# A planned FFT and feed-forward kernel: new piece lengths in its planner, and group 6 prepared tile by tile

## The chip, the core and the metric

The kernel runs on one core of a Trainium2 chip. The metric is the device time of one execution in microseconds (us). Three runs of the kernel before took 1422.62, 1423.76 and 1426.18 us, so the median is 1423.76 us. The profile is of one more execution, which took 1424.53 us; its span, from the first instruction to the last, is 1422.7 us.

## The reference

There are 8 batches of 3136 tokens with 256 channels, all in float32. The reference filters each batch along the tokens in the frequency domain, adds to the result the real part of its two-dimensional Fourier transform, normalizes each token, and sends it through two matrix products with a rectifier between them:

```python
X = np.fft.rfft(x, axis=1)
y = np.fft.irfft(X * (filt_r + 1j * filt_i)[None], n=3136, axis=1)
mixed = np.real(np.fft.fft(np.fft.fft(y, axis=1), axis=2))
u = y + mixed
un = (u - mean(u)) / sqrt(var(u) + 1e-6)
out = u + np.maximum(un @ w_ch1, 0) @ w_ch2    # 256 -> 1024 -> 256
```

## The kernel before

**The stages.** A batch goes through `load_x`, `first` (the first step of the transform, 14 pieces, stored to DRAM as `d1`), `load_at` (`d1` read back turned, 7 pieces, tile `at`), `spectrum` (the second step on TensorE from `at`, then the filter), `inverse1` and `inverse2` (the way back, through DRAM as `d2` and `dy`), and `fold`, which makes the input of the channel transform (`eo`). By symmetry a batch holds 1568 rows of two tokens. The rows of all batches stand in one line and are cut into 49 groups of 256 rows. A group is two tiles of 128 rows, and `pages` holds its tokens.

**A group.** `fetch(g)` reads the group from DRAM. `prepare(g)` mixes the channels on TensorE (`mixing`, the `mix` matmuls of L1081), and adds the result to the group: tile 0 on VectorE (`add`, L1106), tile 1 on GpSimd (`add_plain`, L1131 to L1137, from a copy `sm` that ScalarE makes at L1169). Then come the statistics of each tile (L1246, L1247), the scale and shift in `weigh` (L1215 on ScalarE, L1219 to L1227 on VectorE), and `normalize`, once for each tile: ScalarE writes the normalized tile `un` (L1277), ScalarE and a second engine split it into two float16 halves `u` (L1297 and L1303, GpSimd for most groups), and a DMA transpose on SP's queue turns it into `ut` (L1306). Group 0 goes another way. Its two tiles are finished, weighed and normalized by two tasks of their own (`tile_alone`), and TensorE turns `un` (L1283, `uT`), after which ScalarE and VectorE write the halves straight into `ut` (L1287, L1289). For every other group the one task finishes tile 0, then tile 1, then weighs both together.

**The products.** One task, `products`, runs 8 steps for a group, 392 in all. Step q multiplies the group's `ut` with an eighth of the first weights (`h`, L1328, six matmuls), and then the rectified `h` of two steps before with the second weights (`acc`, L1369, twelve matmuls). It waits for both tiles of `ut` before the first product of a group, so the second products of the last two steps of the group ahead stand behind that wait. `rectify` (L1356 on ScalarE, L1358 on VectorE) turns a first product into the operand of a second one.

**The planner.** No engine chooses its next instruction at run time: each runs its own in the order in which they were written. That order comes from the class `Plan`, which plays the whole kernel through on a clock of its own before anything is built. A task yields an engine and a length (`yield "DVE", 0.65`), and whichever waiting piece has the lowest order number goes next when its engine comes free. `HOP` is the time that the planner adds when a task goes from one engine to another. An SP piece takes its length on the modelled DMA engines. Buffers are rings that a task asks for with `take`. Four banks of PSUM (`psf`) are shared by `first`, `spectrum`, `inverse1`, `inverse2` and the channel mix.

**Order numbers.** Step q of the products has order q. `prepare(g)` has 8g - 19 and `normalize(g, t)` has 8g - 13 + t, so 29 and 35 + t for group 6. The spectra of batch 2 start at 47.45, and step 48 is the first of group 6. Group 6 is the one with the first row of batch 1 in it (row 1568, the group has 1536 to 1791), and its scale factors come from two batches (`alpha_of`, small copies at L1068 and L1070).

## Time and profile before

| | |
|---|---|
| median of three runs | 1423.76 us |
| profiled execution | 1424.53 us |
| span of the profiled execution | 1422.7 us |
| mean granted TensorE clock | 0.972 of full speed |
| TensorE matmuls busy | 1347.1 us, 95% |
| VectorE busy | 1024.7 us, 72% |
| ScalarE busy | 865.0 us, 61% |
| GpSimd busy | 666.5 us, 47% |
| DMA engines, share of 16 | 77.9% |

PE is TensorE's matmuls and PEld its weight loads, DVE is VectorE, ACT ScalarE, POOL GpSimd, and SPq the sequencer that issues the DMAs. A busy share is a mean over stages that have different limits. "idle before <- releaser" says what ended the idle time ahead of an instruction. The granted clock is 1.00 at 2.4 GHz and 0.50 at 1.2 GHz.

### The profile page before, as it was taken

What the parts mean: (1) busy time and instruction counts of PE and PEld (TensorE: products, weight loads), DVE (VectorE), ACT (ScalarE), POOL (GpSimd) and SP (SyncE); (2) the same over time, 40 slices, a digit from 0 to 9 for tenths busy, and PEclk for the clock granted to TensorE, in tenths of its full rate; (3) what the DMA queues carried; (4) which work ended last, traced back from release to release, by engine and by line L of the source; (5) the groups of instructions that cost most, each with busy time, mean ns of one, the idle gap of its engine ahead of it and who ended that gap; (6) DMA issues with size and microseconds to landing.
All of it is one profiled execution on the core that took longest, in us unless ns stands there. A gap on an engine that the chain in (4) does not pass through costs nothing.

```text
span 1422.7 us, 32916 instructions
## 1 busy us (share of the span) xinstructions
PE 1347.1 (95%) x12637; PEld 910.9 (64%) x12637; DVE 1024.7 (72%) x2178; ACT 865.0 (61%) x1647; POOL 666.5 (47%) x827
## 2 busy tenths in 40 slices
PE   5758999969999999999999999999999999999998
PEld 2634666646766676667666666666666676666666
DVE  5687588787778696877779776786968778454543
ACT  4466468746776477756677557755667566444341
POOL 2521295057822585338642675336742597222120
PEclk8767999989999999999999999999999999999999
DMA  9997888887985989689896998669795998544330
GB/s 274 241 285 202 188 187 225 239 211 161 215 224 143 229 192 245 182 183 182 224 209 176 215 226 208 179 163 223 169 262 151 209 207 187 151 109 131 84 78 30
DMA packets 362702, 270.30 MB, mean 190 GB/s; under 512 B 217984, under 2 KB 298320, under 8 KB 362544
## 3 DMA queue, kind: packets, MB, share of 16 engines
q1 hardware_dynamic: 362544, 268.19, 77.9%
q8 instruction: 99, 1.62, 0.5%
q14 instruction: 59, 0.48, 0.1%
HBM read 114.50 MB, written 102.76 MB: 153 GB/s over the span
## 4 chain that ended last, share of the span: by engine, by line
PE 47%; DVE 4%; ACT 2%; DMA 2%; POOL 1%; issue 1%; SPq 1%; POOLq 0%; ACTq 0%; DVEq 0%
PE acc L1369 20%; PE h L1328 19%; PE s L607 2%; PE y L978 2%; PE mix L1081 1%; PE i L890 1%; DMA x<-x 1%; DVE pages L1106 1%; PE s L721 1%; PE s L722 1%; DVE h L1358 1%; DVE st L1246 1%; DMA at<-d 0%; ACT h L1356 0%; DVE x L584 0%
## 5 line engine op out<-in xcount | busy, mean ns | idle before, releaser
L1369 PE MATMUL acc<-w2s,h 128*128 128x256 f16 x4704 | 587.3, 273 | 1.0 <-DVE pages L1383 0.7
L1328 PE MATMUL h<-ut,w1s 128*128 128x512 f16 x2352 | 574.7, 380 | 3.4 <-ACT ut L1287 1.7
L1369 PEld LDWEIGHTS <-h 128*128 128x128 f16 x4704 | 452.1, 98 | 133.0 <-issue 10.9
L1358 DVE SCALAR_TENSOR_TENSOR h<-h,h 128x512 f16<-128x512 f32 x392 | 268.7, 686 | 232.8 <-ACT h L1356 230.6
L1356 ACT ACTIVATE h<-h 128x512 f16<-128x512 f32 x392 | 233.3, 595 | 309.4 <-PE h L1328 299.1
L1328 PEld LDWEIGHTS <-w1s 128*128 128x128 f16 x2352 | 224.5, 98 | 210.4 <-issue 16.6
L1303 POOL TENSOR_TENSOR u<-un,u 128x512 f16<-128x512 f32 x94 | 110.7, 1179 | 315.8 <-ACT u L1297 287.0
L1277 ACT ACTIVATE un<-pages,sb 128x256 f32<-128x256 f32 x196 | 110.9, 596 | 16.7 <-DVE sb L1227 16.6
L1131 POOL TENSOR_TENSOR pages<-sm,pages 128x508 f32<-128x508 f32 x48 | 61.5, 1282 | 112.2 <-ACT sm L1169 78.9
L782 POOL TENSOR_TENSOR late<-yt,late 128x448 f16<-128x448 f32 x98 | 102.8, 1054 | 17.4 <-ACT late L780 16.5
L831 POOL TENSOR_TENSOR eo<-ef,eo 128x448 f16<-128x448 f32 (+6 forms) x62 | 59.6, 966 | 97.0 <-ACT eo L828 68.6
L754 POOL TENSOR_TENSOR yt<-yt,t 128x224 f32<-128x224 f32 x98 | 64.9, 662 | 66.4 <-DVE t L740 51.3
L740 DVE SCALAR_TENSOR_TENSOR t<-s,pF,ft 128x448 f32<-128x448 f32 x126 | 84.0, 675 | 10.2 <-PE s L722 9.7
L1106 DVE SCALAR_TENSOR_TENSOR pages<-mix,alpha,pages 128x254 f32<-128x254 f32 (+2 forms) x188 | 83.9, 478 | 8.9 <-ACT sm L1169 7.5
L1003 ACT ACTIVATE ys<-y,alpha 128x512 f32<-128x512 f32 x110 | 70.9, 683 | 31.8 <-PE y L978 31.6
L1246 DVE BATCH_NORM_STATS2 st<-pages 128x6 f32<-128x256 f32 x196 | 80.5, 411 | 6.5 <-POOL pages L1137 4.9
L740 DVE SCALAR_TENSOR_TENSOR yt<-s,pF,ft 128x448 f32<-128x448 f32 x98 | 66.3, 676 | 25.4 <-PE s L722 22.0
L1383 DVE SCALAR_TENSOR_TENSOR pages<-acc,beta,pages 128x512 f32<-128x512 f32 x98 | 70.4, 743 | 15.7 <-PE acc L1369 15.6
L721 PE MATMUL s<-s,at 112*128 112x56 f16 x896 | 61.5, 190 | 19.9 <-DMA at<-d 17.6
L935 POOL TENSOR_TENSOR bt<-sd,bt 128x512 f16<-128x512 f32 x42 | 48.6, 1159 | 62.7 <-ACT bt L933 62.6
L780 ACT CAST late<-yt 128x448 f16<-128x448 f32 x98 | 55.1, 563 | 33.5 <-POOL yt L756 26.2
L584 DVE SCALAR_TENSOR_TENSOR x<-x,sx,x 112x512 f16<-112x512 f32 x84 | 70.1, 857 | 4.3 <-ACT x L582 4.2
(164 smaller groups left out, 1736.5 us busy)
## 6 DMA issues: line engine op xcount, KB each, us to landing
x<-x SPq DMA_DIRECT2D x56, 448.0 KB
d<-ast SPq DMA_DIRECT2D x112, 224.0 KB
at<-d SPq DMA_DIRECT2D x56, 448.0 KB
pages<-d SPq DMA_DIRECT2D x112, 224.0 KB
out<-pages SPq DMA_DIRECT2D x98, 256.0 KB
pages<-dy SPq DMA_DIRECT2D x92, 256.0 KB
d<-bt SPq DMA_DIRECT2D x98, 224.0 KB
dy<-ys SPq DMA_DIRECT2D x96, 224.0 KB
```

The costliest lines, as they stand in the source:

```text
L721: nc.tensor.matmul(o, w, s2[:, U, 0].rearrange("p (r k) -> p r k", r=2), start=True, stop=False)
L740: nc.vector.scalar_tensor_tensor(out, p, pF[:, 1:2], f, op0=ALU.mult, op1=ALU.mult)
L782: nc.gpsimd.tensor_tensor(y16v[:, 1], yh, y16v[:, 0], op=ALU.subtract)
L1003: nc.scalar.activation(ys[:, 2 * o : 2 * o + 2], p, AF.Copy, scale=alphas[b][:, 2:3])
L1106: nc.vector.scalar_tensor_tensor(out, p, al, y, op0=ALU.mult, op1=ALU.add)
L1246: nc.vector.bn_stats(st[:, 2 * t + k], y[:, t, k])
L1277: nc.scalar.activation(un[:, k], y[:, t, k], AF.Identity, bias=sb[:, i, 1:2], scale=sb[:, i, 3:4])
L1303: nc.gpsimd.tensor_tensor(u16[:, :, :, 1], unv, u16[:, :, :, 0], op=ALU.subtract)
L1328: nc.tensor.matmul(p.rearrange("p (t k q) -> p t k q", t=2, k=2), w1s[:, d, hw, 128 * f : 128 * f + 128], utv[:, :, :, d, hx], start=i == ...
L1356: nc.scalar.activation(h[:, 0], p, AF.Relu)
L1358: nc.vector.scalar_tensor_tensor(h[:, 1], p, 0.0, h[:, 0], op0=ALU.max, op1=ALU.subtract)
L1369: nc.tensor.matmul(acc[:, kind], h[:, hh, c0 : c0 + 128], w2s[:, f, hw], start=f == 0 and kind == 0 and i == 0, stop=f == 7 and kind == 1 ...
```

## The change

Two things are changed. First, the lengths that tasks tell the planner, and `HOP`, get other values. The list is long; most lengths of VectorE and ScalarE go down by 5 to 10%, a few go up, and `HOP` goes from 0.1 to 0.18. These numbers only decide the order in which the instructions are written on each engine and queue; no instruction is added or taken away by them. Second, group 6 is prepared as group 0 is: each of its tiles by a task of its own, with order numbers 13 and 14 (15 and 16 for `normalize`), and turned by TensorE in a bank of the ring `psf`. So for group 6 one `weigh` over four columns becomes two over two columns, and for each tile a ScalarE cast, a GpSimd subtraction and a DMA transpose become four TensorE transposes, a ScalarE copy and a VectorE subtraction. Its ring entry for `ut` is taken before the tiles are finished and not after.

```diff
+ALONE = (0, 6)
+TURNED = (0, 6)
-HOP = 0.1
+HOP = 0.18
...
-            yield "ACT", 0.67
+            yield "ACT", 0.62
...
-            yield "DVE", 0.72
+            yield "DVE", 0.8
...
-            yield "PE", 0.66
+            yield "PE", 0.69
...
-            yield "SP", 1.95, t + max(0, ch - 2)
+            yield "SP", 2.0, t + max(0, ch - 2)
...
-        yield "PE", 0.4 if b else 0.6
+        yield "PE", 0.43 if b else 0.6
...
-        yield "DVE", 0.66
+        yield "DVE", 0.6
...
-            yield "DVE", 0.7
+            yield "DVE", 0.67
...
-        yield "POOL", 1.15
+        yield "POOL", 1.3
...
-            plan.spawn(normalize(g, t, y, sb, ut), -56 + t)
+            plan.spawn(normalize(g, t, y, sb, ut), 8 * g + FIRST + 2 + t - 20 if g else -56 + t)
 
         kt = None
-        if g == 0:
+        if g in ALONE:
             kt = yield take("ut")
             ut = mp.tile([128, 2, 8, 128], F16, tag="ut", name=f"ut_{g}", bufs=2)
             ready[g] = y, ut, kt
             for t in range(2):
-                plan.spawn(tile_alone(t), -55 + t)
+                plan.spawn(tile_alone(t), 8 * g + FIRST - 20 + t if g else -55 + t)
             return
...
-        if g == 0:
-            kp = yield take("pso")
-            pt = ps_o.tile([128, 4, 128], F32, tag="pso", name=f"uT_{t}")
+        if g in TURNED:
+            ring = "psf" if g else "pso"
+            kp = yield take(ring)
+            pt = bank(f"uT_{g}_{t}") if g else ps_o.tile([128, 512], F32, tag="pso", name=f"uT_{t}")
+            pt = pt.rearrange("p (i q) -> p i q", i=4)
             yield "PE", 0.7
...
-                yield "PE", 1.3, q
+                yield "PE", 1.312, q
...
-                    yield "PE", 0.655, q + 0.5
+                    yield "PE", 0.664, q + 0.5
...
-        yield "ACT", 0.54
+        yield "ACT", 0.5
         nc.scalar.activation(h[:, 0], p, AF.Relu)
-        yield "DVE", 0.65
+        yield "DVE", 0.605
```

## Rows read from the trace of the kernel before

**Rows 1.** The head of the page: the span, and the busy time of each engine with its share of the span and its instructions.

```profile
span 1422.7 us, 32916 instructions
...
PE 1347.1 (95%) x12637; PEld 910.9 (64%) x12637; DVE 1024.7 (72%) x2178; ACT 865.0 (61%) x1647; POOL 666.5 (47%) x827
```

**Rows 2.** Busy time by stretches of the span: from and to, its length, busy us and instructions of each engine, the granted clock, the DMA share and GB/s.

```profile
0.00:130.00 130.00, 80.32 (x570) 50.25 (x570) 95.46 (x213) 73.65 (x149) 41.69 (x60) 0.74 0.94 264
130.00:275.00 145.00, 143.16 (x1319) 93.56 (x1319) 113.02 (x227) 97.75 (x185) 65.14 (x84) 1.00 0.84 197
275.00:325.00 50.00, 38.51 (x364) 26.41 (x362) 38.48 (x95) 24.65 (x49) 24.92 (x34) 0.90 0.92 228
325.00:1400.00 1075.00, 1066.04 (x10254) 727.36 (x10252) 770.15 (x1635) 665.20 (x1261) 534.79 (x650) 1.00 0.77 181
```

**Rows 3.** What TensorE waited for between 260 and 340 us: us in total, times, the longest.

```profile
PE s L721 <- DMA at<-d: 9.7, 1, 9.7
PE s L607 <- DVE pages L1106: 1.6, 1, 1.6
```

**Rows 4.** TensorE in order of time from 294 to 314 us: start, length, the operation, and in brackets the idle time before it. The line at 305.34 is the first of the 32 matmuls of two spectra of batch 2, of which the other 31 are left out; 306.83 is the first step of group 6; 309.37 and 312.44 are the last two second products of group 5.

```profile
294.72 0.95 PE L1081 MATMUL mix<-mix,eo 128*128 128x129 f16 x16
305.34 0.23 PE L721 MATMUL s<-s,at 112*128 112x56 f16 x1 [9.66 <-DMA at<-d]
...
306.83 2.74 PE L1328 MATMUL h<-ut,w1s 128*128 128x512 f16 x6
309.37 1.94 PE L1369 MATMUL acc<-w2s,h 128*128 128x256 f16 x12
311.14 1.46 PE L1328 MATMUL h<-ut,w1s 128*128 128x512 f16 x6
312.44 1.47 PE L1369 MATMUL acc<-w2s,h 128*128 128x256 f16 x12
```

**Rows 5.** Busy time in stretches of 2 us, with the columns of rows 2; the third number from the end is the granted clock.

```profile
287.00:289.00 2.00, 0.38 (x3) 0.24 (x3) 1.98 (x5) 0.35 (x1) 0.00 (x0) 1.00 0.38 137
...
299.00:301.00 2.00, 0.00 (x0) 0.00 (x0) 0.80 (x2) 1.10 (x3) 2.00 (x3) 0.77 0.51 133
...
309.00:311.00 2.00, 2.00 (x13) 1.41 (x12) 1.93 (x3) 0.72 (x2) 2.00 (x3) 0.67 1.25 275
311.00:313.00 2.00, 2.00 (x15) 1.21 (x14) 1.97 (x6) 0.93 (x2) 1.05 (x1) 1.00 1.96 230
```

**Rows 6.** VectorE in order of time. 283.55 is the first copy of group 6's factors, 289.13 the first statistics of tile 0 and 293.25 of tile 1, 296.10 the last piece of its `weigh`; 297.27 is the last piece of the first step of batch 2; 309.33 is a piece of `weigh` of group 8.

```profile
283.55 1.09 DVE L1068 COPY al<-alpha 32x2 f32<-32x2 f32 x1
...
289.13 0.42 DVE L1246 BATCH_NORM_STATS2 st<-pages 128x6 f32<-128x256 f32 x1
...
293.25 0.42 DVE L1246 BATCH_NORM_STATS2 st<-pages 128x6 f32<-128x256 f32 x1
...
296.10 0.17 DVE L1227 SCALAR_TENSOR_TENSOR sb<-mv,sb 128x4 f32<-128x4 f32 x1
...
297.27 0.66 DVE L622 TENSOR_TENSOR ast<-s,ast 112x512 f16<-112x512 f32 x1
...
309.33 1.08 DVE L1223 SCALAR_TENSOR_TENSOR sb<-mv,sb 128x4 f32<-128x4 f32 x1
```

**Rows 7.** ScalarE in order of time: the last cast of the first step of batch 2, the square root of group 6, and its two pairs of `un` (tile 0, tile 1).

```profile
291.55 0.61 ACT L617 CAST ast<-s 112x512 f16<-112x512 f32 x1
294.44 0.30 ACT L1215 ACTIVATE sb<-mv,eps 128x4 f32<-128x4 f32 x1 [2.28 <-DVE mv L1247]
...
296.37 1.10 ACT L1277 ACTIVATE un<-pages,sb 128x256 f32<-128x256 f32 x2 [1.14 <-DVE sb L1227]
...
298.02 1.09 ACT L1277 ACTIVATE un<-pages,sb 128x256 f32<-128x256 f32 x2
```

**Rows 8.** GpSimd in order of time: the end of the sum into tile 1 of group 6, the first piece of the sum of group 7, and the subtractions of the two tiles of group 6.

```profile
286.07 0.21 POOL L1137 TENSOR_TENSOR pages<-pages,sm 128x4 f32<-128x4 f32 x1
291.77 1.26 POOL L1131 TENSOR_TENSOR pages<-sm,pages 128x508 f32<-128x508 f32 x1 [5.49 <-ACT sm L1169]
298.19 1.16 POOL L1303 TENSOR_TENSOR u<-un,u 128x512 f16<-128x512 f32 x1 [5.16 <-ACT u L1297]
...
299.99 1.15 POOL L1303 TENSOR_TENSOR u<-un,u 128x512 f16<-128x512 f32 x1
```

**Rows 9.** SP's queue in order of time: the last store of batch 2's `d1`, the two transposes of group 6 with the first load of batch 2's `at` between them, and the two transposes of group 7.

```profile
297.99 0.32 SPq L625 DMA_DIRECT2D d<-ast  x1
299.37 1.25 SPq L1306 DMA_TRANSPOSE ut<-u  x1
300.72 0.52 SPq L653 DMA_DIRECT2D at<-d  x1
301.29 1.33 SPq L1306 DMA_TRANSPOSE ut<-u  x1
...
308.68 5.37 SPq L1306 DMA_TRANSPOSE ut<-u  x2
```

**Rows 10.** Groups of instructions by line and shape: operation, tiles, shapes and count, then busy us, mean ns of one, and the idle time before them. The first is the transposes of group 0.

```profile
L1283 PE MATMUL uT<-ident,un 128*128 128x128 f32 x8 | 2.3, 440 | 2.0 <-ACT un L1277 2.0
L1289 DVE TENSOR_TENSOR ut<-uT,ut 128x512 f16<-128x512 f32 x2 | 1.4, 687 | 0.7 <-ACT ut L1287 0.7
```

More of the change, by code (lines that the diff above doesn't have):

```diff
@@ L539, in measure_x @@
             junk = fp.tile([112, 1024], F16, tag="x16", name=f"xsq_{b}_{q}", bufs=3)
-            yield "ACT", 1.05, t
+            yield "ACT", 1.14, t
             nc.scalar.activation(
@@ L612, in first @@
         st = pool.tile([112, 2, 2, 256], F16, tag=home, name=f"ast_{b}_{q}", bufs=bufs)
-        yield "ACT", 0.53
+        yield "ACT", 0.585
         if wide:
@@ L617, in first @@
             nc.scalar.copy(st[:, :, 0], p)
-        yield "DVE", 0.73 if wide else 0.66
+        yield "DVE", 0.66 if wide else 0.6
         if wide:
@@ L742, in spectrum @@
         filtered(t1, p, fr)
-        yield "DVE", 0.66
+        yield "DVE", 0.6
         filtered(t2, p, fi)
@@ L752, in spectrum @@
         else:
-            yield "POOL", 0.64
+            yield "POOL", 0.62
             nc.gpsimd.tensor_tensor(yh[:, 0], t1v[:, 0], t2v[:, 1], op=ALU.subtract)
-        yield "POOL", 0.64
+        yield "POOL", 0.62
         nc.gpsimd.tensor_tensor(yh[:, 1], t1v[:, 1], t2v[:, 0], op=ALU.add)
@@ L778, in spectrum @@
         yh = yh.rearrange("p r j s q -> p r (j s) q")
-        yield "ACT", 0.51
+        yield "ACT", 0.46
         nc.scalar.copy(y16v[:, 0], yh)
-        yield "POOL", 1.03
+        yield "POOL", 1.01
         nc.gpsimd.tensor_tensor(y16v[:, 1], yh, y16v[:, 0], op=ALU.subtract)
@@ L803, in fold @@
         yt = by_part(b, yts[b, ch][1])
-        yield "POOL", 1.28
+        yield "POOL", 1.24
         for i, o in enumerate((ALU.add, ALU.subtract)):
@@ L807, in fold @@
         if ch == 0:
-            yield "DVE", 0.7
+            yield "DVE", 1.3
             es = tp.tile([128, 2], F32, tag="es", name=f"es_{b}")
@@ L828, in fold @@
             nc.scalar.copy(eo[:, :, 0, r0 : r0 + n], efv[:, :, e0 : e0 + n])
-        yield "POOL", 0.95
+        yield "POOL", 1.0
         for r0, e0, n in parts:
@@ L899, in inverse1 @@
         total = fp.tile([128, 2, 256], F32, tag="x16", name=f"sd_{b}_{ch}", bufs=3)
-        yield "ACT", 0.58
+        yield "ACT", 0.5
         nc.scalar.copy(total, ps[1])
@@ L908, in inverse1 @@
         bt = fp.tile([128, 2, 2, 2, 256], F16, tag="ast", name=f"bt_{b}_{ch}", bufs=3)
-        yield "ACT", 0.55
+        yield "ACT", 0.48
         nc.scalar.copy(bt[:, :, 0, 1], ps[1])
@@ L912, in inverse1 @@
             plan.spawn(low_half(b, ch, kx, total, bt), t)
-        yield "DVE", 0.66
+        yield "DVE", 0.61
         nc.vector.tensor_tensor(bt[:, :, 1, 1], ps[1], bt[:, :, 0, 1], op=ALU.subtract)
@@ L916, in inverse1 @@
         if b == 1:
-            yield "ACT", 0.55
+            yield "ACT", 0.48
             nc.scalar.copy(bt[:, :, 0, 0], ps[0])
-            yield "DVE", 0.66
+            yield "DVE", 0.61
             nc.vector.tensor_tensor(bt[:, :, 1, 0], ps[0], bt[:, :, 0, 0], op=ALU.subtract)
@@ L931, in low_half @@
     def low_half(b, ch, kx, total, bt):
-        yield "ACT", 0.6
+        yield "ACT", 0.52
         nc.scalar.copy(bt[:, :, 0, 0], total)
-        yield "POOL", 1.18
+        yield "POOL", 1.11
         nc.gpsimd.tensor_tensor(bt[:, :, 1, 0], total, bt[:, :, 0, 0], op=ALU.subtract)
@@ L1001, in bring @@
         else:
-            yield "ACT", 0.63
+            yield "ACT", 0.585
             nc.scalar.activation(ys[:, 2 * o : 2 * o + 2], p, AF.Copy, scale=alphas[b][:, 2:3])
@@ L1114, in add @@
         ends = pm[:, 0:129:128].unsqueeze(1).to_broadcast([n, 2, 2])
-        yield "DVE", 0.65
+        yield "DVE", 0.66
         scaled_add(oh[..., 1:], even, al[:, 0:1], oh[..., 1:])
         for hs, sign in ((slice(0, 4, 3), 0), (slice(1, 3), 1)):
-            yield "DVE", 0.4
+            yield "DVE", 0.39
             scaled_add(oh[:, hs, 1:], odd, al[:, sign : sign + 1], oh[:, hs, 1:])
-        yield "DVE", 0.15
+        yield "DVE", 0.14
         scaled_add(o[..., 0:129:128], ends, al[:, 0:1], o[..., 0:129:128])
@@ L1129, in add_plain @@
         ends = sm[:, 0:129:128].unsqueeze(1).to_broadcast([n, 2, 2])
-        yield "POOL", 1.15
+        yield "POOL", 1.3
         nc.gpsimd.tensor_tensor(oh[..., 1:], even, oh[..., 1:], op=ALU.add)
-        yield "POOL", 0.66
+        yield "POOL", 0.69
         nc.gpsimd.tensor_tensor(oh[:, 0:4:3, 1:], oh[:, 0:4:3, 1:], odd, op=ALU.add)
-        yield "POOL", 0.66
+        yield "POOL", 0.69
         nc.gpsimd.tensor_tensor(oh[:, 1:3, 1:], oh[:, 1:3, 1:], odd, op=ALU.subtract)
-        yield "POOL", 0.12
+        yield "POOL", 0.2
         nc.gpsimd.tensor_tensor(o[..., 0:129:128], o[..., 0:129:128], ends, op=ALU.add)
@@ L1167, in mixing @@
                 side["sm"] = fp.tile([128, 256], F32, tag="sm", name=f"sm_{g}", bufs=2)
-                yield "ACT", 0.42
+                yield "ACT", 0.39
                 nc.scalar.activation(side["sm"], pm[:, 1], AF.Copy, scale=al[:, 0:1])
@@ L1213, in weigh @@
         def weigh(part):
-            yield "ACT", 0.25
+            yield "ACT", 0.28
             nc.scalar.activation(sb[:, part, 0], mv[:, part, 1], AF.Sqrt, bias=eps)
@@ L1217, in weigh @@
             r, q, c, s = (sb[:, part, i] for i in range(4))
-            yield "DVE", 0.25
+            yield "DVE", 0.21
             nc.vector.reciprocal(r, r)
-            yield "DVE", 0.25
+            yield "DVE", 0.21
             nc.vector.scalar_tensor_tensor(q, r, -8.0, r, op0=ALU.mult, op1=ALU.mult)
-            yield "DVE", 0.25
+            yield "DVE", 0.21
             nc.vector.scalar_tensor_tensor(c, v, EPS, q, op0=ALU.add, op1=ALU.mult)
-            yield "DVE", 0.25
+            yield "DVE", 0.21
             nc.vector.scalar_tensor_tensor(s, c, 24.0, r, op0=ALU.add, op1=ALU.mult)
-            yield "DVE", 0.25
+            yield "DVE", 0.21
             nc.vector.scalar_tensor_tensor(q, mu, -1.0, s, op0=ALU.mult, op1=ALU.mult)
@@ L1244, in finished @@
             for k in range(2):
-                yield "DVE", 0.5
+                yield "DVE", 0.55
                 nc.vector.bn_stats(st[:, 2 * t + k], y[:, t, k])
@@ L1287, in normalize @@
             nc.scalar.copy(utv[:, :, 0], pt)
-            yield "DVE", 0.65
+            yield "DVE", 0.62
             nc.vector.tensor_tensor(utv[:, :, 1], pt, utv[:, :, 0], op=ALU.subtract)
-            give("pso", kp)
+            give(ring, kp)
             done("ut", g, t)
@@ L1295, in normalize @@
         unv = un.rearrange("p k (d q) -> p k d q", q=128)
-        yield "ACT", 0.56
+        yield "ACT", 0.52
         nc.scalar.copy(u16[:, :, :, 0], unv)
         if g == 1:
-            yield "DVE", 0.65
+            yield "DVE", 0.62
             nc.vector.tensor_tensor(u16[:, :, :, 1], unv, u16[:, :, :, 0], op=ALU.subtract)
         else:
-            yield "POOL", 1.14
+            yield "POOL", 1.11
             nc.gpsimd.tensor_tensor(u16[:, :, :, 1], unv, u16[:, :, :, 0], op=ALU.subtract)
@@ L1381, in finish @@
         k, acc = accs.pop((g, t))
-        yield "DVE", 0.7
+        yield "DVE", 0.66
         nc.vector.scalar_tensor_tensor(y[:, t], acc, beta, y[:, t], op0=ALU.mult, op1=ALU.add)
```

5 lines of the change are left out of this document (2 added, 3 removed).

## The prediction

> **What bounds the kernel now.** I read the head of the page first, then busy time by stages, then what TensorE waited for, and at the one large wait the order of time on each engine. TensorE's matmuls are busy for 95% of the span and no other engine passes 72% [rows 1]. By stages, from 325 to 1400 us TensorE is idle for 1075 - 1066.04 = 8.96 us in all, and from 130 to 275 us for 1.84 us: there the kernel is TensorE's work and little else. The first 130 us lose 49.7 us, but there the DMA engines are busy at a share of 0.94. Between 275 and 325 us TensorE loses 11.49 us at a DMA share of 0.92 [rows 2]. This hole is what the second part of the change touches. Nearly all of it is one wait: 9.66 us before the first spectrum of batch 2, ended by a load of `at`; a wait of 1.6 us lies before it [rows 3].
>
> The releaser named is only the one that came last. In order of time TensorE ends its work at 294.72 + 0.95 = 295.67, starts the two spectra at 305.34, and the first product of group 6 follows at 306.83 with no gap [rows 4]. So both are late: `at` and `ut` of group 6. Group 6 was not ready at 295.67, since its first `un` starts at 296.37 and its second pair at 298.02 [rows 7], the subtractions end at 301.14 [rows 8], and its second transpose is only issued at 301.29 for 1.33 us [rows 9]. Had only `at` been late, products could have filled the time.
>
> The hole costs more than its length. The granted clock is still 1.00 over the idle 1.6 us at 287 us; in the long hole it falls to 0.50 (0.77 is the mean of 299 to 301), and it is back at 1.00 after 311 [rows 5]. In between the first step took from 306.83 to 309.37 and its second products until 311.14, 4.31 us, where the next pair begins its second part 312.44 - 311.14 = 1.30 us after its first [rows 4]; two such parts are about 2.6 us. With the spectra (1.49 us, half of that at the full clock) the low clock costs 1.7 + 0.75 = 2.4 us. The hole is worth 9.66 + 2.4 = 12.1 us.
>
> **The change, part by part.** *Group 6 in two tasks.* Its tile 1 has its sum from GpSimd at 286.28 [rows 8], but its statistics stand at 293.25 in VectorE's order, four microseconds behind those of tile 0 at 289.13 [rows 6], and the square root, which needs both, comes at 294.44 [rows 7]. The planner had put it there, because one task did tile 0 before tile 1. In two tasks with order 13 and 14 the statistics of tile 1 can go first or follow at once. From 293.25 (statistics) to 296.37 + 1.10 = 297.47 (a tile's `un` done) is 4.22 us in this trace [rows 6, 7]. Tile 0 may then have its `un` at 289.13 + 4.22 = 293.35. Four statistics pieces of the other tile (293.25 to the square root at 294.44, so 1.2 us) may stand ahead of it, which gives 294.55; the other tile follows by one pair of `un`, 1.1 us: 295.65.
>
> *Turned by TensorE.* Four transposes at 440 ns mean are 1.0 to 1.8 us in the half-clocked stretch of group 0 [rows 10]; I take 1.0, since they overlap. The ScalarE copy (0.6, as its casts [rows 7]) and the VectorE subtraction (0.69 [rows 10]) come after: 2.3 us behind `un`. So `ut` is complete between 293.35 + 1.1 + 2.3 = 296.75 (nothing of the other tile's statistics ahead) and 295.65 + 2.3 + 0.9 = 298.85, where the 0.9 is one small piece held up as the one at 309.33 was (1.08 for 0.17 [rows 6]); I take 298.0. In exchange go two casts, two subtractions of 1.16 us, and two issues on SP of 1.25 and 1.33 us. VectorE gets more: two subtractions (1.4) and five small pieces of a second `weigh` (5 x 0.17): 2.2 us. What stands behind these on VectorE is the last piece of batch 2's first step: its ScalarE cast ends at 292.16 [rows 7], and it runs at 297.27 [rows 6]. Its store, 0.7 us later, then opens the loads of `at` at 300.72 [rows 9]. So `at` can come later by up to 2.2 us, or earlier by up to the 1.25 us of the transpose that was issued ahead of it. The eight transposes on TensorE (2.0 to 2.4 us) lie in time when it has nothing else. They add a wait, though: whatever the planner writes behind a transpose stands until its `un` is there. Group 0's transposes waited 2.0 us [rows 10]. Behind group 6's stand the last products of group 5 at worst; 0 to 2.0 us, and I take 0, since 298.0 - 2.3 for their start is later than the 295.67 at which that work is done.
>
> *The sum.* The first product of group 6 then starts at about 298.0 after an idle time of some 2.3 us, with less than that where the transposes fill it; the clock should hold, by the 1.6 us that did no harm. Before, at 312.44, one step of group 6 and its second products, the two spectra and one more step were done. In the new order that takes 298.0 + 3 x 1.30 + 0.75 = 302.65: 9.8 us less. I take off 1.0 for spectra that the planner may put ahead of their data (`at` came at 305.34, and now there are products to run until then) and 0.3 for `uT` in a bank that `first` and the mix also want (the 1.6 us wait of rows 3 is such a one). That leaves 8.5 us. The ends are 0 (nothing fills the hole) and 12.1.
>
> *The lengths.* They change no instruction, only places. That the old ones were off can be seen at a small piece of `weigh`, planned at 0.25 us, which takes 0.17 [rows 6]; it gets 0.21. What they can win is bounded by the idle time outside the start and the hole, 8.96 + 1.84 = 10.8 us [rows 2]; what they can lose is a second wait like this one, 12.1 us. I take 0: a plan drawn anew moves small waits without a sign. The start is bound by DMA, so I give it 0 as well, with 2 us to either side.
>
> After 325 us TensorE has hardly a gap, so what is won at 300 us is kept if the data keep up. Next late would be group 7: GpSimd's sum for it started at 291.77 and stood still until group 6's first subtraction at 298.19 was through [rows 8]; without these subtractions it ends earlier. Its transposes, issued from 308.68 on [rows 9], have until 298.0 + 8 x 2.6 = 318.8.
>
> *A rule against it.* A small piece of `weigh` took 1.08 us at 309.33, beside GpSimd's work, against 0.17 at 296.10, and a copy of two columns 1.09 us [rows 6]. The Trainium skill (SBUF — State Buffer, "SBUF: two separate sides") says that VectorE and GpSimd share one port pair as a lock, which a VectorE operation with two inputs in SBUF waits for as long as a GpSimd instruction runs. The trace agrees. By this rule group 7's sum, now moved up beside group 6's two `weigh`, could hold them through all its pieces (case 2 below), where the rows alone give the 0.9 us that stands in the sum.
>
> **The rivals.** The profiled execution took 1424.53, 0.8 us over the median; I give times as medians.
>
> 1. *Forecast:* 8.5 us less, 1423.8 - 8.5 = 1415.3. Its own range is 1411 to 1420. Chance 0.46.
> 2. *GpSimd holds `weigh`.* The sum of group 7 (a first piece of 1.26 us and three more [rows 8], together some 2.5) stops VectorE in its new place: `ut` is 2.5 us later, 1417.8. For it, rows 6; against it, only one piece of five was held there. Chance 0.06.
> 3. *The lengths win too,* half of the 10.8 us: 1410. For it, the planner's order is the only cause of waits such as tile 1's statistics; against it, the small waits are short and scattered. Chance 0.12.
> 4. *Won and given back.* Batch 2 goes through DMA, whose share is 1.25 to 1.96 around 310 us [rows 5]; products run ahead and then wait for it. Half is lost: 1419.5 to 1421, at most 1424. Against it, the share from 325 on is 0.77 [rows 2]. Chance 0.16.
> 5. *The change does not do what it says.* The planner still writes the spectra ahead of group 6's first product: TensorE waits for `at`, which VectorE's added 2.2 us make later, less up to 1.25 on SP: 0.9 to 2.2 us slower, and with the low clock that lasts as long, up to 1428. It decides as soon as the spectra stand first. Against it: their order 47.45 is below 48, but `ut` is now ready some 7 us ahead of `at`. Chance 0.10.
> 6. *Slower:* the new order makes such a wait at another batch (five more come, each with its spectra right after a load of `at`): 9.66 + 2.4 = 12.1 us, net 3.6 slower, 1427.4; and 1439 with two. It decides once a spectrum stands 6.1 us ahead of its data, since 6.1 + 2.4 eats up the 8.5 won. Against it: after 325 us all idle time together is 9 us. Chance 0.10.
>
> **How the numbers follow.** 0.3% is 4.3 us, about what can be told from no change: faster is below 1419.5, slower above 1428.0. Faster: 0.43 of case 1, 0.06, 0.12 and 0.04 of case 4, 0.65. The same: 0.03 of case 1, 0.11 of case 4, 0.06 of case 5 and 0.03 of case 6, 0.23. Slower: 0.01, 0.04 and 0.07 of cases 4 to 6, 0.12. The range from 1408 to 1426 leaves out half of case 3 and most of the last two, under 0.2.
>
> **What would show it.** Right: the first product of group 6 between 296 and 300 us, ahead of the spectra; the wait for `at` gone or under 2 us; the clock at 1.00 all through 295 to 311; TensorE's idle time in 275 to 325 down from 11.5 to 3 or 4 us, and the span shorter by as much and 2 us more. Wrong: the spectra still ahead of that product, or a wait over 5 us at another batch, or a first stage that ends more than 3 us later.

## The result and the profile after

The changed kernel is slower. It takes 1432.46 us (median of 4 runs, 1431.36 to 1433.55) against 1423.4 us for the kernel before, run beside it, a ratio of 1.006 with a 95% interval of 1.0043 to 1.0078. The forecast was 1415.3 us. Its profiled execution took 1433.55 us. Two executions, one of the kernel before at 1769.64 us and the profiled one of `e4_pe_old` at 7833.35 us, lie far outside all others; they move no median below by more than 0.3 us.

The head of the page and the busy time by stages of the changed kernel answer to [rows 1, 2]:

```profile
span 1431.7 us, 32945 instructions
...
PE 1351.3 (94%) x12645; PEld 911.0 (64%) x12645; DVE 1033.8 (72%) x2185; ACT 864.6 (60%) x1648; POOL 662.2 (46%) x825
```

```profile
0.00:130.00 130.00, 79.51 (x554) 49.04 (x555) 94.00 (x202) 70.86 (x141) 40.88 (x60) 0.74 0.92 262
130.00:275.00 145.00, 138.41 (x1225) 89.56 (x1227) 108.71 (x228) 93.51 (x180) 64.89 (x84) 0.98 0.79 183
275.00:325.00 50.00, 45.22 (x433) 30.22 (x422) 40.98 (x94) 28.46 (x54) 12.18 (x17) 1.00 0.79 216
325.00:1400.00 1075.00, 1060.29 (x10249) 722.78 (x10248) 780.50 (x1649) 665.83 (x1266) 544.26 (x665) 1.00 0.78 183
```

TensorE's idle time is the length of a stretch less the first busy number. It changed like this:

```
stretch (us)     before   after   change
0 to 130          49.68   50.49    +0.8
130 to 275         1.84    6.59    +4.75
275 to 325        11.49    4.78    -6.7
325 to 1400        8.96   14.71    +5.75
```

The hole that group 6 was to close is indeed smaller by 6.7 us. Two stretches that had hardly any idle time gained 10.5 us. With the 4.2 us that TensorE is busier (1351.3 against 1347.1) this is the longer span: 0.8 + 4.75 - 6.7 + 5.75 + 4.2 = 8.8 of 9.0 us. Of the 4.2 us the eight transposes of group 6 take 0.93 + 0.38 + 0.44 = 1.75. The clock takes about 1.4: matmuls are busy for 46.8 us at a clock of 0.50, against 44.1 before, and half of the difference is lost. The rest was not traced to a place.

**Where along the run.** The start of the first product of a group is a milestone, since the 392 steps come in the same order in every version; other work can stand ahead of it in one version and behind it in another. A profile is of one execution. Those of the two kernels, `e1_group6` and `e2_lengths` lie within 1.1 us of their medians, those of `e8`, `e13` and `e17` 4 to 5.5 us off, so a shift of a few us, at the start above all, can be chance. Against the kernel before, the changed kernel stands like this:

```
group                   0      4      5      6      7     14     29     36     48
start before (us)  119.09 231.57 256.84 306.83 333.58 522.49 925.07 1111.39 1395.41
after, later by      +2.5   +4.8  +12.1   +1.9   +0.1   +1.6   +4.2   +8.6   +8.9
```

Four things can be read from it: 4.8 us later up to group 4, 7.3 more just ahead of group 5, 10.2 won back at group 6 (its first product starts at 308.77 us), and, from group 7 on, 8.8 lost bit by bit up to the end.

**Ahead of group 5.** TensorE in order of time (start, length, operation, and in brackets the idle time before it):

```profile
262.07 0.38 PE L428 MATMUL pb_x<-row_x,ones 1*128 1x2 f32 x2 [0.93 <-DVE row_x L565]
263.49 0.58 PE L609 MATMUL s<-x,s 112*112 112x512 f16 x1 [1.04 <-ACT x L584]
264.27 4.85 PE L609 MATMUL s<-x,s 112*112 112x512 f16 x11 [0.21 <-DVE x L586]
268.92 1.99 PE L1332 MATMUL h<-ut,w1s 128*128 128x512 f16 x6
```

SP's queue over the same time, first of the changed kernel, then of the kernel before:

```profile
258.04 1.26 SPq L1310 DMA_TRANSPOSE ut<-u  x1
...
264.73 1.27 SPq L1310 DMA_TRANSPOSE ut<-u  x1
```

```profile
250.22 3.83 SPq L1306 DMA_TRANSPOSE ut<-u  x2
```

Group 5's two transposes were issued together at 250.22 before. Now the first comes at 258.04 and the second at 264.73. TensorE meets the scale factors of batch 2 and its `first` pieces instead, waits 0.93 + 1.04 + 0.21 = 2.2 us for them (in the kernel before it waited 1.20 us for the scale factors at this place), and then does twelve of these matmuls at half the clock, as the 2 us stretches show (third number from the end):

```profile
263.00:265.00 2.00, 1.31 (x3) 0.56 (x3) 1.97 (x6) 1.66 (x3) 0.21 (x1) 0.54 0.41 113
265.00:267.00 2.00, 2.00 (x6) 1.09 (x5) 1.60 (x3) 1.60 (x3) 0.00 (x0) 0.50 0.83 178
267.00:269.00 2.00, 2.00 (x6) 0.89 (x6) 1.42 (x3) 1.31 (x4) 0.00 (x0) 0.50 0.73 174
```

At 261.14 the last product of group 4 ended, and group 5 starts at 268.92. Not all of this is lost: in the kernel before the `first` pieces stand behind the first step of group 5, where nine such matmuls took 2.11 us. That part of the 7.3 us is work moved ahead, and it is also part of the 10.2 us that come back by group 6.

**The second products.** What TensorE waited for over the whole run (us in total, times, longest), the changed kernel first and then the kernel before:

```profile
PE acc L1373 <- DVE pages L1387: 10.1, 14, 2.0
PE s L723 <- DMA at<-d: 8.7, 4, 5.1
```

```profile
PE s L721 <- DMA at<-d: 17.6, 4, 9.7
...
PE acc L1369 <- DVE pages L1383: 0.7, 2, 0.4
```

The load of `at` costs 8.9 us less. But the second products now wait 14 times, 10.1 us in all, for VectorE to add the ones before them to `pages` (`finish`, below "finish waits"); before it was 0.7 us. Of the 10.1 us, 8.2 lie after 325 us, where TensorE's idle time grew by 5.75. They are the largest new wait there. That they are the loss is not shown by this, and two kernels of the next section (`e2_lengths`, `e6_vec_more`) speak against it.

### The profile page after: what moved, and what is told of

Same layout as the page of the kernel before. It is cut to its first block, busy times and chain, and to the rows that moved or that the text cites. A ratio compares the mean times of both kernels' runs of the same rounds, so it can differ in the third digit from the quotient of the medians.

```text
span 1431.7 us, 32945 instructions
## 1 busy us (share of the span) xinstructions
PE 1351.3 (94%) x12645; PEld 911.0 (64%) x12645; DVE 1033.8 (72%) x2185; ACT 864.6 (60%) x1648; POOL 662.2 (46%) x825
## 4 chain that ended last, share of the span: by engine, by line
PE 52%; DVE 8%; DMA 3%; ACT 2%; issue 2%; POOL 2%; SPq 1%; DVEq 0%; POOLq 0%; ACTq 0%
PE acc L1373 22%; PE h L1332 22%; PE y L980 2%; PE s L609 2%; PE mix L1083 1%; PE i L892 1%; DVE h L1362 1%; DVE pages L1108 1%; DMA d<-ast 1%; DVE st L1248 1%; DVE pages L1387 1%; PE s L723 1%; PE s L724 1%; DMA at<-d 1%; DMA dy<-ys 1%
## 5 line engine op out<-in xcount | busy, mean ns | idle before, releaser
L1373 PE MATMUL acc<-w2s,h 128*128 128x256 f16 x4704 | 589.2, 273 | 10.3 <-DVE pages L1387 10.1
L808 POOL TENSOR_TENSOR ef<-yt 128x224 f32<-128x224 f32 x112 | 73.6, 678 | 0.2
L980 PE MATMUL y<-pages,i2f 56*64 56x256 f16 (+1 forms) x1288 | 57.2, 299 | 15.6 <-issue 11.5
```

The costliest lines, as they stand in the source:

```text
L980: nc.tensor.matmul(ps[o][64 * h : 64 * h + 64, js], table[row, e], bt[row, half, lx, turn], start=i == 0 and js == 0, stop=i == len(passes ...
L1373: nc.tensor.matmul(acc[:, kind], h[:, hh, c0 : c0 + 128], w2s[:, f, hw], start=f == 0 and kind == 0 and i == 0, stop=f == 7 and kind == 1 ...
```

## The experiments

All times are medians, and a ratio is against the kernel before, run beside it, with its 95% interval. Theories go by letters in the expectations: A is that the two parts have opposite signs, B that the hole only moves, C is the longer `HOP`, D less slack in the lengths of VectorE and ScalarE, E TensorE's lengths, F that any newly drawn order loses here, H the direction of `HOP`, I that the order of before is an ordinary one, and J that the new lengths do badly in a whole neighbourhood.

**The parts apart.** `e1_group6` is the kernel before with the group 6 part only; `e2_lengths` is the change without it.

```diff
 # e1_group6, against the kernel before: lengths and HOP stay
+ALONE = (0, 6)
+TURNED = (0, 6)
...
 # e2_lengths, against the kernel after
-ALONE = (0, 6)
-TURNED = (0, 6)
+ALONE = (0,)
+TURNED = (0,)
```

> Group 6 in two tasks and turned by TensorE, with all the old lengths and HOP 0.1. Theory A (the two parts of the change have opposite signs: group 6 wins what was forecast, the lengths lose more than that): 8 to 11 us faster than before, 1413 to 1416 us, the first product of group 6 near 297 to 300 us. Theory B (the hole is only moved: any new order opens a like hole at a neighbouring group): within 4 us of before, 1420 to 1428.

> All new lengths and HOP 0.18, group 6 prepared as before the change. Theory A: 14 to 20 us slower than before, 1438 to 1444 us, with the waits of the second products for finish (about 10 us in the changed kernel) and a late group 5 still there. Theory B: 1424 to 1434 us, no slower than the changed kernel.

Group 6 alone takes 1418.38 us, 0.9957 [0.9937, 0.9976]; the lengths alone take 1435.53 us, 1.0079 [1.0053, 1.0106]. The signs are those of A; both effects are smaller than A gave (8 to 11 us won, 14 to 20 lost). TensorE in order of time in the first of them, around group 6, and that stage's busy time:

```profile
289.20 1.46 PE L609 MATMUL s<-x,s 112*112 112x512 f16 x6
292.41 0.93 PE L1287 MATMUL uT<-ident,un 128*128 128x128 f32 x4 [1.75 <-ACT un L1279]
293.18 1.47 PE L1373 MATMUL acc<-w2s,h 128*128 128x256 f16 x12
295.18 0.63 PE L1287 MATMUL uT<-ident,un 128*128 128x128 f32 x4 [0.53 <-ACT un L1279]
...
296.48 0.38 PE L1332 MATMUL h<-ut,w1s 128*128 128x512 f16 x1
297.93 1.24 PE L1332 MATMUL h<-ut,w1s 128*128 128x512 f16 x5 [1.07 <-DVE ut L1293]
```

```profile
275.00:325.00 50.00, 46.59 (x467) 32.24 (x466) 43.65 (x107) 29.00 (x59) 23.10 (x32) 1.00 0.87 219
```

The first product of group 6 starts at 296.48, 10.4 us earlier than before; the idle time of the stage is 3.41 us, and its clock 1.00. At the end of the run 6.7 us are left. With the new lengths alone the hole is still there (idle 12.35 us, clock 0.86), and finish waits come to 6.5 us:

```profile
275.00:325.00 50.00, 37.65 (x364) 24.95 (x363) 39.66 (x90) 26.46 (x51) 18.69 (x24) 0.86 0.99 241
325.00:1400.00 1075.00, 1065.79 (x10264) 726.81 (x10263) 773.79 (x1643) 663.13 (x1266) 536.96 (x659) 1.00 0.78 183
```

```profile
PE acc L1369 <- DVE pages L1383: 6.5, 11, 2.2
```

The starts of the groups, against the kernel before (us later by):

```
group              0      4      5      6      7     14     29     36     48
e1_group6       -0.8   -0.8   -0.9  -10.4  -11.7  -10.3  -19.0   -6.7   -6.7
e2_lengths      +2.9   +5.3  +10.3  +10.2  +10.5   +8.9  +12.3  +11.5  +10.8
change          +2.5   +4.8  +12.1   +1.9   +0.1   +1.6   +4.2   +8.6   +8.9
```

The lengths by themselves lose nearly everything ahead of group 5. From 325 to 1400 us TensorE is idle for 9.21 us with them, as it was before (8.96), though 4.3 us of finish waits lie there. And less than half of the loss is idle time:

```profile
PE 1353.7 (94%) x12637; PEld 912.6 (64%) x12637; DVE 1027.2 (72%) x2178; ACT 862.5 (60%) x1647; POOL 662.4 (46%) x827
```

The same 12637 matmuls are busy 6.6 us longer (1347.1 before), and idle time grew by 4.2 us (79.8 against 75.6). Most of the 6.6 us is the clock. After 130 us the matmuls are busy for 14.7 us at 0.50, against 5.0 before, and half of the difference is lost: 4.9 us. It stands at 0.50 behind a finish wait of 2.20 us at 188.8, again behind the waits for batch 2's scale factors and `first` pieces (0.93, 1.04 and 0.41 us from 260.5 on), and behind the hole:

```profile
190.00:192.00 2.00, 2.00 (x27) 1.48 (x24) 2.00 (x5) 1.81 (x4) 1.93 (x4) 0.50 0.57 205
```

So the lengths lose what the other part wins, and 4.3 us more (10.7 - 6.4). The change loses 9.1 us, 4.7 more than the two parts do apart. Up to group 7 they add up: -11.7 and +10.5 make -1.2, and the change stands at +0.1. Behind it the change loses 8.8 us, where the parts lose 5.0 and 0.3. What makes them lose more together there is not shown.

**Which lengths.** Both take one group of values back in the changed kernel.

```diff
 # e3_hop_old
-HOP = 0.18
+HOP = 0.1
...
 # e4_pe_old
-            yield "PE", 0.69
+            yield "PE", 0.66
...
-        yield "PE", 0.43 if b else 0.6
+        yield "PE", 0.4 if b else 0.6
...
-                yield "PE", 1.312, q
+                yield "PE", 1.3, q
...
-                    yield "PE", 0.664, q + 0.5
+                    yield "PE", 0.655, q + 0.5
```

> The changed kernel with HOP back at 0.1, all other new lengths kept. Theory C (of the new numbers it is HOP that spoils the order): 1414 to 1418 us and the waits for finish under 3 us. Theory D (it is the lower lengths of VectorE and ScalarE: the planner now packs these engines with less slack than they need): 1432 to 1440 us, no better than the changed kernel.

> The changed kernel with the four lengths of TensorE back at their old values (1.3, 0.655, 0.66, 0.4), the rest new. Theory E (the planner's TensorE is now slower than the real one, 2.64 for a step that takes 2.605 us, so that other engines come late to it): 1416 to 1424 us, waits for finish under 4 us. Theories C and D: 1430 to 1435 us, the waits for finish stay near 10 us.

`HOP` alone put back changes nothing for the better: 1435.63 us, 1.0076 [1.005, 1.0102]. C falls. TensorE's four lengths put back give 1426.18 us, 1.0013 [0.9994, 1.0031], 6.3 us less than the change. The time is between what E gave (1416 to 1424) and what C and D gave (1430 to 1435). Its profile is of the execution of 7833 us, so whether its finish waits went is not seen.

**Slack, or any change at all.** The next four keep the group 6 part and the old lengths (the 1418.4 us kernel) and alter what the planner reckons with.

```diff
 # e5_vec_less; e6_vec_more has 1.07
+        length *= 0.93 if engine in ('DVE', 'ACT') else 1
...
 # e7_pe_more
+        length *= 1.011 if engine in ('PE',) else 1
...
 # e8_hop_hair
-HOP = 0.1
+HOP = 0.11
```

> Group 6 as changed, old lengths, but the planner multiplies every length of VectorE and ScalarE by 0.93, about what the new lengths do to these engines. Theory D (less slack on these engines makes real pieces come late to their places): 5 to 10 us slower than the run with group 6 alone (1418.4 us), 1423 to 1429 us, and over 5 us of waits of second products for finish. Theory F (the order of before is a lucky one, and any new order loses some us, whatever the sign of the edit): slower too, by 2 to 10 us.

> The same, multiplied by 1.07 in place of 0.93, so that the planner sees fuller engines than before. Theory D: no slower than group 6 alone, 1414 to 1419 us, waits for finish at or under 3 us. Theory F: slower by 2 to 10 us, 1420 to 1428.

> Group 6 as changed, old lengths, but every length of TensorE times 1.011, about what the new lengths do to it (2.61 to 2.64 for a step). Theory E (a planner whose TensorE is slower than the real one sends the other engines late): 4 to 8 us slower than group 6 alone, 1422 to 1427 us. Theory D: 1416 to 1420. Theory F: slower by 2 to 10 us.

> Group 6 as changed, old lengths, HOP 0.11 in place of 0.10: an edit too small to mean anything, which still draws a new order. Theory F: 2 to 10 us slower than group 6 alone, 1420 to 1428 us, with the loss in other places than in the other runs. Theories D and E: within 2 us of it, 1416 to 1420.

Shorter lengths of VectorE and ScalarE give 1440.96 us, 1.0113 [1.0086, 1.0139]: a loss, as D wants, but of 22 us where it gave 5 to 10, and with finish waits of 4.2 us where it gave over 5. Longer ones give 1447.54, 1.0156 [1.0126, 1.0185], where D wanted no loss. As a matter of slack D is gone. This slowest of all kernels has finish waits of 1.0 us: they are no measure of what an order loses. TensorE's lengths 1.1% up give 1433.65, 1.0062 [1.0042, 1.0083], with finish waits of 7.3 us:

```profile
PE acc L1374 <- DVE pages L1388: 7.3, 9, 1.3
```

E has the sign of this and not the size (15 us over `e1_group6`, 4 to 8 expected). But `HOP` 0.01 up, which touches no length of TensorE, gives 1434.26 us (9 runs, 1429.6 to 1439.5), 1.0072 [1.0054, 1.009], 16 us over the kernel it differs from by this hair. F stands in its sign; all four losses are larger than the 2 to 10 us that it gave.

**Is it the order of before that was lucky?**

```diff
 # e9_hop_less, group 6 and old lengths
-HOP = 0.1
+HOP = 0.09
...
 # e10_before_hair, the kernel before
-HOP = 0.1
+HOP = 0.11
...
 # e11_hair_len, group 6 and old lengths
+        length *= 1.002 if engine in ('DVE', 'ACT') else 1
...
 # e12_group5, the kernel after
-ALONE = (0, 6)
-TURNED = (0, 6)
+ALONE = (0, 5, 6)
+TURNED = (0, 5, 6)
```

> Group 6 as changed, old lengths, HOP 0.09: a hair to the other side. Theory F (the lengths of before were picked by their time, so that nearly any other order loses, to either side and by an amount that the edit's size does not set): 1424 to 1440 us, slower than group 6 alone (1418.4) by more than 4. Theory H (more hop time makes the order worse, less makes it better): 1414 to 1419 us.

> The kernel before with HOP 0.11 and nothing else. Theory F: 5 to 20 us slower than before, 1430 to 1445 us, though no instruction is added; with the run of group 6 and HOP 0.11 (1434 us) it gives the worth of the group 6 part in a third order: that part should still win 2 to 10 us, so 1436 to 1444. Theory I (before is an ordinary order, and only orders with group 6 turned are touchy): within 3 us of before.

> Group 6 as changed, old lengths, VectorE's and ScalarE's lengths times 1.002 for the planner. Theory F: slower than group 6 alone by 3 to 25 us, 1421 to 1443. Theory D in its other reading (the size of the edit sets the loss, 22 us for 0.93 and 29 for 1.07): under 2 us, 1417 to 1421.

> The changed kernel with group 5 prepared tile by tile and turned by TensorE as well. Its hole before group 5 (the first product of group 5 at 268.9 us, 12 us later than before) is the one that the new order opened. If the local reading is right, the first product of group 5 comes at 256 to 262 us and the time falls to 1422 to 1428 us. Theory F adds that this is one more order: 1420 to 1440 us with other holes, even when group 5 is on time.

`HOP` 0.01 down also loses: 1432.66, 1.0052 [1.0033, 1.007], so H falls. The kernel before with the same hair up takes 1443.45, 1.0126 [1.0101, 1.015], 18 us lost with no instruction changed. Its finish waits are 3.7 us. The largest of its waits that is new is one for `ut`, 8.4 us in three times, where the kernel before has 0.3 us:

```profile
PE h L1328 <- DMA ut<-u: 8.4, 3, 5.6
```

I falls with this. `e8_hop_hair`, the same hair with group 6 turned, has 7.7 us of this wait. But lengths of VectorE and ScalarE 0.2% up leave the good order good: 1417.53, 0.9946 [0.9931, 0.9961], which F did not have (1421 to 1443) and D's other reading had, by which the size of the edit sets the loss. "Any" is too strong a word in F.

With group 5 turned by TensorE too, its first product starts at 263.58 (256 to 262 was expected) and not at 268.92, and the step from group 4 to group 5 costs nothing (+6.9, then +6.7 us against the kernel before). So this hole goes when group 5's tiles come early, which fits the late second transpose above. The time is 1435.94 all the same, 1.0081 [1.005, 1.0112], where 1422 to 1428 was expected: the redrawn order loses 2 us more at the start and 11.9 after group 7.

**Neighbourhoods.** The last six are hairs around the changed kernel (`e13` to `e16`) and around the good one (`e17`, `e18`).

```diff
 # e13_new_hop17; e14_new_hop19 has 0.19
-HOP = 0.18
+HOP = 0.17
...
 # e15_new_up, the kernel after; e16_new_down has 0.998
+        length *= 1.002 if engine in ('DVE', 'ACT') else 1
...
 # e17_old_down, group 6 and old lengths
+        length *= 0.998 if engine in ('DVE', 'ACT') else 1
...
 # e18_old_hop105, group 6 and old lengths
-HOP = 0.1
+HOP = 0.105
```

> The changed kernel with HOP 0.17 in place of 0.18: an order a hair from it. Theory F (ordinary orders spread over some 20 us, and the new lengths are no better and no worse than the old ones): anywhere from 1417 to 1440 us. Theory J (the new lengths are worse by themselves): 1430 to 1440 us, as the changed kernel.

> The changed kernel with HOP 0.19. Theory F: anywhere from 1417 to 1440 us. Theory J: 1430 to 1440 us.

> The changed kernel, VectorE's and ScalarE's lengths times 1.002 for the planner. Theory F: anywhere from 1417 to 1440 us; of the four new orders at least one under 1427. Theory J: 1430 to 1440 us, none of the four under 1427.

> The changed kernel, VectorE's and ScalarE's lengths times 0.998 for the planner. Theory F: anywhere from 1417 to 1440 us. Theory J: 1430 to 1440 us.

> Group 6 as changed, old lengths, VectorE's and ScalarE's lengths times 0.998 for the planner. Theory F: anywhere from 1417 to 1440 us. Theory J: near the two good orders of the old lengths or between them and the others, 1417 to 1430 us.

> Group 6 as changed, old lengths, HOP 0.105. Theory F: anywhere from 1417 to 1440 us. Theory J: 1417 to 1434 us.

```
new lengths, with group 6    us      ratio [95%]              finish waits (us)
after                     1432.46  1.0060 [1.0043, 1.0078]    10.1
e13 HOP 0.17              1433.46  1.0053 [1.0033, 1.0072]     9.8
e14 HOP 0.19              1438.99  1.0095 [1.0071, 1.0119]     8.9
e15 DVE, ACT x 1.002      1431.39  1.0038 [1.0020, 1.0056]     7.7
e16 DVE, ACT x 0.998      1432.52  1.0047 [1.0024, 1.0070]     5.7
old lengths, with group 6
e1                        1418.38  0.9957 [0.9937, 0.9976]     2.6
e11 DVE, ACT x 1.002      1417.53  0.9946 [0.9931, 0.9961]     3.3
e17 DVE, ACT x 0.998      1420.25  0.9962 [0.9944, 0.9980]     2.6
e18 HOP 0.105             1419.17  0.9954 [0.9938, 0.9970]     2.3
e8  HOP 0.11              1434.26  1.0072 [1.0054, 1.0090]     4.1
e9  HOP 0.09              1432.66  1.0052 [1.0033, 1.0070]     1.7
```

The five orders from the new lengths are all slower than the kernel before; none is under 1431, where F gave at least one of the four hairs under 1427. Of the six from the old lengths four are near 1419 and two are near 1433. J holds in this: around the new lengths no good order turned up, around the old ones most are good. It holds with a limit: orders a hair apart share much of their course, so five of them are not five independent draws, and the two bad ones of the old lengths lie in the same band. How much is shared can be counted in the traces, as the part of VectorE's instructions that are followed by the same one. With `e1_group6` the good hairs `e11`, `e17` and `e18` share 67, 70 and 75%, the bad ones `e8` and `e9` 69 and 70%. So a bad hair does not change the order more than a good one, and D's other reading is not borne out by this.

The two bad bands are not bad in the same way. In all five of the upper ones finish waits are 5.7 to 10.1 us, and group 4 starts 4.4 to 7.5 us late. Of the two lower ones `e9_hop_less` has finish waits of 1.7 us, with group 4 5.6 us late and group 48 9.7. `e8_hop_hair` has 4.1, and its group 36 still starts 2.0 us earlier than in the kernel before; group 44 starts 5.0 later, behind the longer (5.1 us) of its two waits for `ut`. That one loses late, at another wait (its profiled execution lies 4.7 us under its median).

**The fastest** are `e1_group6` and the three good ones of its five hairs, 1417.5 to 1420.3 us: the group 6 part without the new lengths beats both kernels, by 6 us and by 14.

## Why the prediction was wrong

**What bounds the kernel: right.** The hole at 295 us was `ut` of group 6 as well as `at`. With `ut` early and `at` no earlier (its load was issued at 300.86 us in `e1_group6`, at 300.72 before), TensorE worked through it.

**Group 6 in two tasks, turned by TensorE: right with this part alone.** Forecast for the first product 298.0, measured 296.48 in that kernel; forecast 9.8 us less at that place, measured 10.4 there. In the changed kernel it comes at 308.77, since group 5 was late; the 10.2 us won from group 5 to group 6 (+12.1 to +1.9) hold some work that was only moved. The clock of 1.00 through the stage came as said, and the idle time of 3.41 us as well ("3 or 4"). The new wait on the transposes, taken at 0, was 1.75 + 0.53 us in front of group 6, inside the 2.3 us that the prediction gave to idle time there. Case 5 did not come: in neither kernel do spectra stand ahead of that product. Case 2 did not come with this part alone: there all pieces of group 6's two `weigh` take 0.15 or 0.16 us. It did come in the changed kernel, where VectorE's pieces of the first `weigh` stand beside GpSimd's sum of group 7:

```profile
301.45 0.91 DVE L1223 SCALAR_TENSOR_TENSOR sb<-sb 128x2 f32<-128x2 f32 x1
302.59 0.57 DVE L1227 SCALAR_TENSOR_TENSOR sb<-sb 128x2 f32<-128x2 f32 x1
303.20 0.65 DVE L1229 SCALAR_TENSOR_TENSOR sb<-mv,sb 128x2 f32<-128x2 f32 x1
```

```profile
301.08 1.26 POOL L1133 TENSOR_TENSOR pages<-sm,pages 128x508 f32<-128x508 f32 x1 [4.78 <-ACT sm L1171]
302.42 0.73 POOL L1135 TENSOR_TENSOR pages<-pages,sm 128x254 f32<-128x254 f32 x1
303.11 0.72 POOL L1137 TENSOR_TENSOR pages<-pages,sm 128x254 f32<-128x254 f32 x1
```

Three pieces are held there, for 1.65 us together, where the prediction's sum had 0.9 and its case 2 had 2.5. What this did to the time was not measured by itself.

**The end of the run: a size off.** The step took off 1.3 us and left 8.5. Alone the part is worth 6.4 us (1424.8 - 1418.38), so 4 of the 10.4 us were given back, where 1.3 were taken off. That is case 4's kind of loss, of over a third and not of half. Its place was not batch 2's DMA: group 14 still starts 10.3 us earlier than before, group 29 even 19.0 (products went ahead of other work there), and group 36 6.7, as does group 48. So it was given back between groups 14 and 36. Between 900 and 1010 us the profile shows a new wait of 2.8 us for VectorE's split of `x`, and then the clock at 0.50; the second wait is in the kernel before as well, with the same 1.5 us:

```profile
PE s L609 <- DVE x L586: 2.8, 1, 2.8
...
PE mix L1083 <- DVE sd L907: 1.5, 1, 1.5
```

```profile
940.00:945.00 5.00, 3.75 (x10) 1.49 (x10) 1.89 (x3) 3.95 (x8) 2.31 (x2) 0.50 0.97 269
```

Matmuls are busy for 5.5 us at that clock, of which half is lost: 2.8 + 2.7 = 5.5 us, against 5.0 lost in this profile from group 7 (-11.7) to the end (-6.7). In other orders the same part is worth 1.7 to 3.1 us (`e2_lengths` to the change, by the difference to the kernel before or by the times) and 9.2 (`e10_before_hair` to `e8_hop_hair`).

**The lengths: the step that failed.** The prediction said "I take 0: a plan drawn anew moves small waits without a sign". Measured by themselves, the lengths cost 10.7 us (1435.53 - 1424.8). Its two bounds, 10.8 us to win and 12.1 to lose, held the value by luck, since 12.1 was the price of one wait like the hole and the loss is no such wait; `e6_vec_more` lost 29 us against `e1_group6`. What was wrong is "without a sign": the order of the kernel before is a good one by its trace (1.84 us idle from 130 to 275 us, 8.96 from 325 to 1400), so a new plan has little to win and much to lose. Eighteen kernels here, the change among them, have other lengths or another `HOP` than the kernel before: fourteen are slower by more than 0.3%, one cannot be told from it, and the three that are faster differ from it, beside group 6, by 0.2% or 0.005.

Where they cost, by `e2_lengths`: 2.9 us at the start, which the 2 us to either side do not quite hold; 2.4 up to group 4; and 5.0 just ahead of group 5, at a place that no case named. Of it all 4.2 us are idle time and about 5 the clock, which fell behind waits of at most 2.2 us and stayed low longer behind the hole; the prediction had a price for the low clock only behind a hole like this one. In the changed kernel group 6 then wins its 10 us, and 8.8 more are lost behind group 7. There 8.2 us of finish waits, 13 of at most 1.2 us, are the largest new wait. **Case 6 named the kind (won at group 6, lost at another place) and put it at a spectrum that waits for `at`.** That wait did not come: `at` costs 8.7 us in the changed kernel and 17.6 before. The sign "a wait over 5 us at another batch" did not show the loss either.

In the sum, then: the group 6 part was put at 8.5 us won and is worth 6.4 by itself, and the lengths were put at 0 and lose 10.7. That makes 4.3 us slower; the other 4.7 us of the 9.1 come from both together, since the group 6 part is worth only 1.7 to 3.1 us on top of the new lengths.

**How one finish wait comes about.** VectorE in order of time from 184 to 190 us in the changed kernel, and below it GpSimd and TensorE:

```profile
184.30 0.73 DVE L1223 SCALAR_TENSOR_TENSOR sb<-sb 128x4 f32<-128x4 f32 x1
185.07 0.97 DVE L1225 SCALAR_TENSOR_TENSOR sb<-mv,sb 128x4 f32<-128x4 f32 x1
186.07 0.97 DVE L1227 SCALAR_TENSOR_TENSOR sb<-sb 128x4 f32<-128x4 f32 x1
187.08 0.17 DVE L1229 SCALAR_TENSOR_TENSOR sb<-mv,sb 128x4 f32<-128x4 f32 x1
...
189.15 0.74 DVE L1387 SCALAR_TENSOR_TENSOR pages<-acc,beta,pages 128x512 f32<-128x512 f32 x1
```

```profile
183.73 1.28 POOL L808 TENSOR_TENSOR ef<-yt 128x224 f32<-128x224 f32 x2
184.96 2.07 POOL L784 TENSOR_TENSOR late<-yt,late 128x448 f16<-128x448 f32 x2
```

```profile
186.51 1.46 PE L1332 MATMUL h<-ut,w1s 128*128 128x512 f16 x6
189.94 0.81 PE L1373 MATMUL acc<-w2s,h 128*128 128x256 f16 x6 [1.97 <-DVE pages L1387]
```

The order puts `weigh` and pieces of a spectrum ahead of `finish` on VectorE. Three pieces of `weigh` take 0.73, 0.97 and 0.97 us where the last takes 0.17; they end at 185.03, 186.04 and 187.04, and GpSimd's instructions beside them at 185.01, about 186.0, and 187.03. `finish` comes at 189.15, and TensorE has stood for 1.97 us. In the kernel before, VectorE's `finish` ran at 184.44 and `weigh` behind it, from 191.26 on: there the same pieces were held as well (1.00 and 0.98 us) and TensorE did not wait for them.

```profile
184.44 1.40 DVE L1383 SCALAR_TENSOR_TENSOR pages<-acc,beta,pages 128x512 f32<-128x512 f32 x2
...
191.46 1.00 DVE L1221 SCALAR_TENSOR_TENSOR sb<-sb 128x4 f32<-128x4 f32 x1
```

So the rule of the Trainium skill that the prediction weighed (SBUF — State Buffer, "SBUF: two separate sides") agrees with this trace, to within 0.04 us at each end. Without the hold these three pieces would have taken 2.2 us less, which is more than the wait. In the 6 us ahead of seven of the 14 waits, 7.2 of the 10.1 us, VectorE has two to four held pieces, 1.4 to 2.4 us longer together than free ones; ahead of the other seven, of at most 0.6 us each, it has none. That the hold is the cause is argued from this and not shown for each. Nor does it set the time of a kernel: 36 pieces are held in the kernel before, 55 in the changed one and 53 in `e2_lengths`, but 50 in `e11_hair_len`, the fastest, and 33 in `e6_vec_more`, the slowest.

**Open.** Which of the lengths makes the order worse is settled in part: TensorE's four lengths back win 6.3 us, and 1.1% on TensorE's lengths alone bring finish waits of 7.3 us. What in the planner leads from the one to the other was not shown, nor was VectorE's and ScalarE's new set tried without TensorE's and without the group 6 part. Nor is it shown that the new lengths are worse at all than the old ones in a wide sense: 5 bad orders of 5 against 2 of 6, hairs of one another, say no more than that the old values were the better find.

## What to carry to other kernels

Where the order of every engine is drawn by a planner, a value that only the planner reads is an edit of the whole kernel. Price it by the idle time that is left (little to win) against what a redrawn order costs here (5 to 22 us against the kernel before in 14 of 18 draws, which are not independent), and not at nothing. Count the low clock behind each new wait as well as the wait. Lengths that are truer to the trace are no aim in themselves (and TensorE's went the other way here: a step, 2.60 us in the trace, went from 2.61 to 2.64 in the planner): keep the old ones when a local part is changed, try some hairs around each set, and choose by measured time.

## What was not expected of the hardware

A `weigh` piece beside GpSimd lasts until GpSimd's instruction ends, wherever in it it begins: 0.73 us when begun 0.7 us ahead of that end, 0.97 when begun 0.96 ahead; alone it is 0.17. All 55 held pieces of the changed kernel (those of two inputs that take over 0.25 us) end within 0.03 us of the end of a GpSimd instruction.

The clock of TensorE was at 1.00 through idle times of 1.75 us and 1.07 us at 291 and 297 us in the kernel with the group 6 part alone. In the changed kernel it fell to 0.54 at 263 to 265 us, after 0.93 and 1.04 us idle with a matmul of 0.38 us in between, and stayed at 0.50 for 4 us in which TensorE was busy all the time. In `e2_lengths` it fell behind a finish wait of 2.20 us; behind the one of 1.97 us in the changed kernel it did not. So "the 1.6 us that did no harm", on which the prediction rested, is no bound for two shorter ones close together.
